# Loading w1 in two transfers and making h1 in two passes, with w2's large blocks in front of its small transfers

## The chip, the cores and the metric

The kernel runs on one core of one Trainium2 chip. The metric is device time in microseconds (us) for one execution. Before the change it is 670.66 us, the median of 3 runs (670.47 to 671.0).

## The reference: one decode step of attention and a small MLP

Four sequences (B = 4) each decode one token of width D = 640. There are two parts, each behind a layer norm and each added to its input:

```
h  = x + A(layernorm(x))        A: q = ln(x) @ wq, 32 heads of 128, softmax(q k^T / sqrt(128)) v, then @ wo
out = h + B(layernorm(h))       B: h1 = ln(h) @ w1 + b1;  act = h1 * tanh(softplus(h1));  act @ w2
```

The cached keys and values have 4096 positions for each of 32 heads and 4 sequences, in bf16: they make nearly all of the 283 MB that are read. w1 is 640 x 1728 (2160 KB), w2 is 1728 x 640. The change lies in part B alone.

## The kernel before, in words

**Attention.** The work is cut into NG = 32 groups; a group is four heads of one sequence. `load_k` and `load_v` (line 98) fetch 4 MB of keys and 4 MB of values for a group into two buffers each. For every group VectorE multiplies the keys by the query (line 348), TensorE sums the products with an identity matrix (line 355), VectorE finishes the sums (line 367), ScalarE makes the exponentials (line 398), and TensorE multiplies them by the values (line 255). Groups overlap: the values of group g - 1 are used while the keys of group g are multiplied. The last group's values come in four transfers of 1 MB (VP = 4).

All loads are issued by SyncE (SP) in program order. The schedule is written out by hand: each engine executes its instructions in the order in which the program names them.

**The loads of part B** stand behind the group loop. `w12` is one tile in the key buffer that group 30 leaves; its first columns are `w1_sb` (5 row blocks of 128 rows, side by side: `p c f`), and the rest is `w2_sb`, three large blocks of w2 (640 KB each, four rows of w2 to a partition). What is left of w2 goes to two small tiles, `w2s_sb` (128 rows, 160 KB) and `w2r_sb` (64 rows, 80 KB). SP issues w1 whole (line 476), w2s (line 477), w2r (line 478), and then the three blocks of w2 (line 480).

**The end of attention** comes next: the last exponentials, the last products with the values (lines 255 and 282), the normalisation (line 305), the last part of the product with wo (line 329), and the sum with x, `hT` (line 505). All of this holds the activations transposed, 640 features as five blocks of 128 partitions by 4 sequences.

**The MLP.** `column_means` (lines 509 and 513) gives the mean; `h2T` and `hc` are the centred activations (line 520). The product with w1 (line 534) takes h2T before it is divided by the standard deviation; that division follows later. It has FC = 14 chunks of columns: 13 of 128 and a last one, `C2`, of 64. For each chunk five matmuls (dc = 0 to 4, one for each row block of w1) sum into four columns of `h1_ps`. So the first chunk already needs all of w1. Chunks 0 to 11 read w1's columns with a stride of four elements (`f_chunk`), chunks 12 and 13 read them side by side. After chunk 4 come the two float32 matmuls of the variance (line 513); ScalarE takes its square root (line 544) and loads the table of the exponential (line 547). Then a chain without overlap runs: VectorE scales and adds b1 (lines 550, 557), ScalarE's exponential (line 565), and four VectorE instructions (lines 567 to 581) give `act_t`. The product with w2 (line 596) has 70 matmuls that sum into `y2T`: w2s first, then w2r, then the twelve chunks of the large blocks. The residual (line 604), a transposition (line 611), a copy (line 619) and the store (line 620) end the kernel.

Of the kernel before, what the change touches and what calls it, by code (L numbers as in the profile page):

```python
# [8 lines left out]
FP32 = mybir.dt.float32  # L9
BF16 = mybir.dt.bfloat16  # L10
ACT = mybir.ActivationFunctionType
# [5 lines left out]
def kernel(  # L17
# [24 lines left out]
    nc = tc.nc  # L42
# [3 lines left out]
    F = B_w1.shape[1]  # L46
    N = B * Sq
    DC = D // 128
# [19 lines left out]
    CI = 4  # L68
    CK = F // (128 * CI)
    FM = CK * CI * 128  # L70
    C2 = F // 128
    FREM = F - C2 * 128
    FC = C2 + 1

    ctx.enter_context(tc.manual_schedule())

# [49 lines left out]
    eps_t = consts.tile([128, 1], FP32)  # L126
# [9 lines left out]
    nc.gpsimd.memset(rs2[:, :, :], 0.0)  # L136
    b1T = consts.tile([128, FC], FP32)
    nc.gpsimd.memset(b1T[:, :], 0.0)
    otn = consts.tile([128, HQ, N, G], BF16)

    for q in range(G):
        nc.vector.tensor_copy(
            out=sel[:, :, q, q * PH : (q + 1) * PH],
            in_=ident[0:N, 0:N].unsqueeze(2).to_broadcast([N, N, PH]),
# [81 lines left out]
    for hq in Q_AT[-1]:  # L226
# [12 lines left out]
        out=pick[:, :],  # L239
        in_=ident_f[:, :].rearrange("p (t i) -> p i t", t=T)[:, 0 : J * G, :],  # L240
# [73 lines left out]
    def f_chunk(rows, c):  # L314

        if c < CK * CI:
            k, i = divmod(c, CI)
            block = rows[:, k * 128 * CI : (k + 1) * 128 * CI]
            return block.rearrange("p (f i) -> p i f", i=CI)[:, i, :], 128
        return rows[:, c * 128 : min(F, (c + 1) * 128)], min(F - c * 128, 128)  # L320
# [87 lines left out]
    for g in range(NG):  # L408
# [33 lines left out]
        if g in WO_AT:  # L442

            if not wo_sb:
# [3 lines left out]
                out=wo_sb[0][:, h0 : h0 + WOC, :],  # L448
                in_=A_wo.rearrange("(h p) n -> p h n", p=128)[:, h0 : h0 + WOC, :],
# [3 lines left out]
        if g == B1_AT:  # L453
            b_ps = ps.tile([128, FC], FP32, tag="small", name="b_ps")
            for c in range(FC):
                cols, fw = f_chunk(b1_row[:, :], c)
                nc.tensor.matmul(
                    b_ps[0:fw, c : c + 1],
                    lhsT=cols,
                    rhs=ident[0:1, 0:1],  # L460
                    start=True,
                    stop=True,
                )
            nc.vector.tensor_copy(out=b1T[:, 0:C2], in_=b_ps[:, 0:C2])
            nc.vector.tensor_copy(out=b1T[0:FREM, C2:FC], in_=b_ps[0:FREM, C2:FC])


    mlp = ctx.enter_context(tc.tile_pool(name="mlp", bufs=1))
    w12 = kpool.tile([128, DC * F + CK * CI * D], BF16, tag="kt", name="w12")
    w1_sb = w12[:, 0 : DC * F].rearrange("p (c f) -> p c f", c=DC)  # L470
    w2_sb = w12[:, DC * F :].rearrange("p (k i n) -> p k i n", k=CK, i=CI)
    w2s_sb = mlp.tile([128, D], BF16)
    w2r_sb = mlp.tile([FREM, D], BF16)

    w2_view = B_w2[0:FM, :].rearrange("(k p i) n -> p k i n", k=CK, i=CI)
    nc.sync.dma_start(out=w1_sb, in_=B_w1.rearrange("(c p) n -> p c n", p=128))
    nc.sync.dma_start(out=w2s_sb[:, :], in_=B_w2[FM : C2 * 128, :])
    nc.sync.dma_start(out=w2r_sb[:, :], in_=B_w2[C2 * 128 : F, :])
    for k in range(CK):
        nc.sync.dma_start(out=w2_sb[:, k], in_=w2_view[:, k])  # L480

    h1_ps = ps.tile([128, FC, N], FP32, tag="qq", name="h1_ps")
    nc.vector.memset(h1_ps[FREM:128, FC - 1, :], 0.0)

# [15 lines left out]
    dummy = consts.tile([N, 1], FP32)  # L500
# [6 lines left out]
    def column_means(src, name):  # L507
        part = mlp.tile([128, N], FP32, name=f"{name}_part")
        nc.vector.tensor_reduce(
            out=part[:, :], in_=src[:, :, :].rearrange("p c n -> p n c"), axis=AX.X, op=ALU.add  # L510
        )
        m_ps = ps.tile([128, N], FP32, tag="small", name=f"{name}_ps")
        nc.tensor.matmul(m_ps[:, :], lhsT=mean_f[:, :], rhs=part[:, :], start=True, stop=True)
        return m_ps

    m_ps = column_means(hT, "mean")
    h2T = mlp.tile([128, DC, N], BF16)
    hc = mlp.tile([128, DC, N], FP32)
    for dst in (h2T, hc):
        nc.vector.tensor_tensor(  # L520
            out=dst[:, :, :],
# [4 lines left out]
    sq = mlp.tile([128, DC, N], FP32)  # L526
# [1 line left out]


    rstd = mlp.tile([128, N], FP32)  # L530
    for c in range(FC):
        fw = f_chunk(w1_sb[:, 0, :], c)[1]
        for dc in range(DC):
            nc.tensor.matmul(  # L534
                h1_ps[0:fw, c, :],
                lhsT=f_chunk(w1_sb[:, dc, :], c)[0],
                rhs=h2T[:, dc, :],
                start=(dc == 0),
                stop=(dc == DC - 1),
            )  # L540
        if c == 4:
            v_ps = column_means(sq, "var")
            std = mlp.tile([128, N], FP32)
            nc.scalar.activation(
                out=std[:, :], in_=v_ps[:, :], func=ACT.Sqrt, bias=eps_t[:, :], scale=1.0
            )
            nc.scalar.activation(out=dummy[:, :], in_=eps_t[0:N, :], func=ACT.Exp)
            nc.vector.reciprocal(out=rstd[:, :], in_=std[:, :])
    h1n = mlp.tile([128, FC, N], FP32)
    nc.vector.tensor_tensor(  # L550
        out=h1n[:, :, :],
# [6 lines left out]
        out=h1s[:, :, :],  # L558
# [9 lines left out]
        out=tb[:, :, :],  # L568
# [8 lines left out]
        out=ta[:, :, :], in0=tb[:, :, :], scalar1=-0.5, scalar2=-1.0, op0=ALU.mult, op1=ALU.add  # L577
# [4 lines left out]
        out=act_t[:, :, :],  # L582
# [5 lines left out]
    )  # L588

    y2T = ps.tile([128, DC, N], FP32, tag="ot", name="y2T")  # L590
    w2_of = [(w2s_sb[:, :], CK * CI), (w2r_sb[:, :], C2)]
    w2_of += [(w2_sb[:, c // CI, c % CI, :], c) for c in range(CK * CI)]
    for i, (w2, c) in enumerate(w2_of):
        rows = 128 if c < C2 else FREM
        for dc in range(DC):
            nc.tensor.matmul(  # L596
                y2T[:, dc, :],
                lhsT=w2[:, dc * 128 : (dc + 1) * 128],
                rhs=act_t[0:rows, c, :],
                start=(i == 0 and dc == 0),  # L600
                stop=(i == FC - 1 and dc == DC - 1),
# [3 lines left out]
        out=oT[:, :, :].rearrange("p n c -> p c n"),  # L605
# [7 lines left out]
        lhsT=oT[:, :, :].rearrange("p n c -> p (n c)"),  # L613
        rhs=ident[:, :],
        start=True,
        stop=True,
# [35 lines left out]
```

## Time and profile before

| What | Value |
|---|---|
| median of 3 runs | 670.66 us (670.47 to 671.0) |
| time of the profiled execution | 670.71 us |
| its span, first to last instruction | 668.9 us |
| granted TensorE clock, mean | 0.838 |
| read from HBM | 283.35 MB, 424 GB/s over the span |
| busy share: TensorE, VectorE, ScalarE | 66%, 53%, 17% |

The span leaves out 1.81 us of the time of the profiled execution, which lie around the first and the last instruction. All places in time below count from the start of the span. In an instruction's row the first number is its start, the second the time that the group took, "xN" the number of instructions in it; "SPq" is SP issuing a transfer, and a row "DMA" in the chain of waits is the time from the issue of a transfer to its landing.

### The profile page before, as it was taken

How to read it: one execution, taken by the hardware profiler on the slowest of the kernel's cores; microseconds unless marked ns; L12 is line 12 of the kernel's file. 1: busy time of each engine (PE TensorE's matmuls, PEld its weight loads, DVE VectorE, ACT ScalarE, POOL GpSimd, SP SyncE). 2: the span in 40 equal slices, each digit the busy share in tenths (PEclk: the TensorE clock that was granted, in tenths of full speed). 3: DMA queues.
4: the chain of work that ended last, by engine and by line, in shares of the span. 5: the costliest groups of instructions: out<-in, count | busy, mean ns of one | idle time of the engine just before them, and what ended most of it. 6: DMA issues, size and time to landing. Idle time of an engine off the chain costs nothing.

```text
span 668.9 us, 6865 instructions
## 1 busy us (share of the span) xinstructions
PE 440.6 (66%) x2969; PEld 200.7 (30%) x2969; DVE 353.0 (53%) x306; ACT 113.8 (17%) x345; POOL 2.4 (0%) x13
## 2 busy tenths in 40 slices
PE   0588777887667475367666857757555875667775
PEld 0233333343222232133222323323222332223335
DVE  2486445556655356236654545657454566545732
ACT  0022122131111111011110111111011121111131
POOL 1000000000000000000000000000000000000000
PEclk9997889797777886797777789778788797788985
DMA  9999999999999999999999999999999999999995
GB/s 375 437 436 435 424 429 437 434 434 427 430 437 432 427 422 418 443 423 434 431 428 433 434 436 430 427 433 436 434 431 428 435 434 435 436 426 426 436 415 211
DMA packets 15478, 283.80 MB, mean 424 GB/s; under 512 B 1299, under 2 KB 5591, under 8 KB 6616
## 3 DMA queue, kind: packets, MB, share of 16 engines
q1 hardware_dynamic: 15440, 283.36, 98.8%
q8 instruction: 23, 0.38, 0.2%
q14 instruction: 7, 0.06, 0.0%
q10 hardware_dynamic: 8, 0.01, 0.0%
HBM read 283.35 MB, written 0.01 MB: 424 GB/s over the span
## 4 chain that ended last, share of the span: by engine, by line
DMA 63%; DVE 17%; PE 17%; issue 1%; SPq 0%; ACT 0%; DVEq 0%
DMA kt<-in_A_k_cache_dram 59%; DVE kt L348 15%; PE s L355 14%; DMA w<-in_B_w_dram 4%; DVE s_sb L367 2%; PE tr L380 1%; PE p_ps L255 1%; PE h_ps L534 0%; DVE mx L385 0%; PE q_ps L193 0%; PE tr L393 0%; PE y2T L596 0%; PE qb_ps L207 0%; SPq L98 0%; ACT q_all L200 0%
## 5 line engine op out<-in xcount | busy, mean ns | idle before, releaser
L355 PE MATMUL s<-kt,ident 128*128 128x512 bf16 x1024 | 296.8, 442 | 196.3 <-DVE kt L348 193.1
L348 DVE TENSOR_TENSOR kt<-kt,qbs 128x4096 bf16<-128x4096 bf16 x128 | 291.5, 2279 | 240.1 <-DMA kt<-in_A_k_cache_dram 240.1
L355 PEld LDWEIGHTS <-ident 128*128 128x128 bf16 x1024 | 110.1, 111 | 342.2 <-issue 170.6
L398 ACT ACTIVATE e<-s_sb,nbs 32x128 bf16<-32x128 f32 x128 | 74.0, 578 | 2.5
L255 PE MATMUL p_ps<-vt,e 128*16 128x512 bf16 x1016 | 64.5, 397 | 1.2 <-DMA vt<-in_A_v_cache_dram 1.2
L395 ACT COPY nbs<-tr 128x4 f32<-128x4 f32 x32 | 5.2, 162 | 331.2 <-PE tr L393 331.2
L265 ACT COPY p_sb<-p_ps 128x512 f32<-128x512 f32 x32 | 18.8, 586 | 159.7 <-PE p_ps L255 159.7
L367 DVE TENSOR_REDUCE s_sb<-s 128x64 f32<-128x512 f32 x64 | 43.5, 680 | 3.8 <-PE s L355 3.8
L271 PEld LDWEIGHTS ot<-pick,p_sb 128*128 128x128 f32 x256 | 34.3, 196 | 6.2 <-ACT p_sb L265 1.9
L255 PEld LDWEIGHTS <-e 128*16 128x16 bf16 x1016 | 23.1, 91 | 40.2 <-issue 20.0
L398 ACT ACTIVATION_READ_ACCUMULATOR e<-s_sb,nbs 32x1 f32 x128 | 32.2, 252 | 0.0
L271 PE MATMUL ot<-pick,p_sb 128*128 128x4 f32 x256 | 31.4, 246 | 0.9 <-ACT p_sb L265 0.7
L385 DVE TENSOR_REDUCE mx<-tr 1x4 f32<-1x128 f32 x32 | 8.9, 278 | 24.3 <-PE tr L380 24.3
L193 PE MATMUL q_ps<-wq_sb,xT 128*4 128x512 bf16 x40 | 11.0, 409 | 9.8 <-DMA wq_sb<-in_A_wq_dram 9.8
L380 PE MATMUL tr<-ident_f,pm 128*1 128x128 f32 x64 | 15.6, 335 | 1.2 <-DVE pm L378 1.2
L393 PEld LDWEIGHTS tr<-mx,nscale 1*128 1x128 f32 x64 | 9.4, 182 | 13.8 <-issue 12.3
L302 DVE RECIPROCAL rl<-l_ps 128x16 f32<-128x16 f32 x8 | 2.1, 258 | 21.0 <-PE l_ps L294 21.0
L207 PE MATMUL qb_ps<-q_all,sel 4*128 4x128 bf16 x128 | 9.2, 225 | 5.3 <-ACT q_all L200 5.3
L393 PE MATMUL tr<-mx,nscale 1*128 1x4 f32 x64 | 12.2, 258 | 0.4 <-DVE mx L385 0.4
L207 PEld LDWEIGHTS <-sel 4*128 4x128 bf16 x128 | 8.4, 98 | 9.1 <-issue 9.1
L200 ACT CAST q_all<-q_ps 4x512 bf16<-4x512 f32 x8 | 4.6, 575 | 35.0 <-PE q_ps L193 35.0
L380 PEld LDWEIGHTS tr<-ident_f,pm 128*1 128x1 f32 x64 | 2.8, 81 | 23.3 <-issue 23.3
(81 smaller groups left out, 69.5 us busy)
## 6 DMA issues: line engine op xcount, KB each, us to landing
kt<-in_A_k_cache_dram SPq DMA_DIRECT2D x31, 4096.0 KB, 25.2
vt<-in_A_v_cache_dram SPq DMA_DIRECT2D x31, 4096.0 KB, 32.8
wq_sb<-in_A_wq_dram SPq DMA_DIRECT2D x1, 5120.0 KB
wo_sb<-in_A_wo_dram SPq DMA_DIRECT2D x4, 1280.0 KB, 30.1
kt<-in_A_k_cache_dram SPq DMA_DIRECT2D x2, 2048.0 KB, 17.5
vt<-in_A_v_cache_dram SPq DMA_DIRECT2D x4, 1024.0 KB, 20.1
w<-in_B_w_dram SPq DMA_DIRECT2D x1, 2160.0 KB, 28.3
w<-in_B_w_dram SPq DMA_DIRECT2D x3, 640.0 KB, 16.0
```

The lines of the kernel that those rows point to most:

```text
L193: nc.tensor.matmul(q_ps[:, :], lhsT=xT[:, c, :], rhs=wq_sb[:, c, n * QC : (n + 1) * QC], start=(c == 0), stop=(c == DC - 1),)
L207: nc.tensor.matmul(qb_ps[:, b * Dh : (b + 1) * Dh], lhsT=sel[:, b, q, :], rhs=q_all[:, h * Dh : (h + 1) * Dh], start=(q == 0), stop=(q == ...
L255: nc.tensor.matmul(p_ps[c0 : c0 + J * G, :], lhsT=e2[g % NE2][:, r : r + J, :].rearrange("p j q -> p (j q)"), rhs=vts[g][:, r : r + J, :]. ...
L265: nc.scalar.copy(out=blocks[g][:, :], in_=p_ps[:, :])
L271: nc.tensor.matmul(o, lhsT=p_sb[:, j * Dh : (j + 1) * Dh], rhs=pick[:, j * G : (j + 1) * G], start=(j == 0), stop=(stop and j == J - 1),)
L348: nc.vector.tensor_tensor(out=kt[:, :, d0 : d0 + DQ], in0=kt[:, :, d0 : d0 + DQ], in1=qbs[:, hq, b, d0 : d0 + DQ].unsqueeze(1).to_broadcas ...
L355: nc.tensor.matmul(s_ps[:, :, :], lhsT=ident[:, :], rhs=kt[:, :, d : d + W], start=(d == 0), stop=(d == Dh - W),)
L367: nc.vector.tensor_reduce(out=s_sbs[g][:, part * RP : (part + 1) * RP], in_=s_of.pop((g, part))[:, :, :], axis=AX.X, op=ALU.add,)
L380: nc.tensor.matmul(tr_ps[0:1, 0:128], lhsT=pm[:, :], rhs=ident_f[:, :], start=True, stop=True)
L385: nc.vector.tensor_reduce(out=mx[:, :], in_=tr_ps[0:1, 0:128].rearrange("o (a b) -> o a b", a=G), axis=AX.X, op=ALU.max,)
L393: nc.tensor.matmul(nb_ps, lhsT=nscale[:, :], rhs=mx[:, :], start=True, stop=True)
L398: nc.scalar.activation(out=e2[g % NE2][p0:p1, :, q], in_=s_sb[p0:p1, :], func=ACT.Exp, bias=nb[p0:p1, q : q + 1], scale=SCALE, accum_out=r ...
```

## The change

w1 is loaded in two transfers, row blocks 0 to 2 (1296 KB) and 3 to 4 (864 KB). h1 is made in two passes over all chunks, the first with row blocks 0 to 2, the second with 3 and 4; both sum into the same columns of `h1_ps`, and now only the first matmul of all has the start mark and only the last has the stop mark. In each pass the chunk of 64 columns comes second, behind chunk 0. The variance stays behind chunk 4, in the first pass. SP issues the three large blocks of w2 in front of w2r and w2s, and the product with w2 takes them in that order.

```diff
+    W1_PARTS = ((0, 3), (3, DC))
...
-    nc.sync.dma_start(out=w1_sb, in_=B_w1.rearrange("(c p) n -> p c n", p=128))
-    nc.sync.dma_start(out=w2s_sb[:, :], in_=B_w2[FM : C2 * 128, :])
-    nc.sync.dma_start(out=w2r_sb[:, :], in_=B_w2[C2 * 128 : F, :])
+    w1_view = B_w1.rearrange("(c p) n -> p c n", p=128)
+    for c0, c1 in W1_PARTS:
+        nc.sync.dma_start(out=w1_sb[:, c0:c1], in_=w1_view[:, c0:c1])
     for k in range(CK):
         nc.sync.dma_start(out=w2_sb[:, k], in_=w2_view[:, k])
+
+    nc.sync.dma_start(out=w2r_sb[:, :], in_=B_w2[C2 * 128 : F, :])
+    nc.sync.dma_start(out=w2s_sb[:, :], in_=B_w2[FM : C2 * 128, :])
...
-    for c in range(FC):
-        fw = f_chunk(w1_sb[:, 0, :], c)[1]
-        for dc in range(DC):
-            nc.tensor.matmul(
-                h1_ps[0:fw, c, :],
-                lhsT=f_chunk(w1_sb[:, dc, :], c)[0],
-                rhs=h2T[:, dc, :],
-                start=(dc == 0),
-                stop=(dc == DC - 1),
-            )
-        if c == 4:
-            v_ps = column_means(sq, "var")
...
+    for c0, c1 in W1_PARTS:
+        for c in (0, C2, *range(1, C2)):
+            fw = f_chunk(w1_sb[:, 0, :], c)[1]
+            for dc in range(c0, c1):
+                nc.tensor.matmul(
+                    h1_ps[0:fw, c, :],
+                    lhsT=f_chunk(w1_sb[:, dc, :], c)[0],
+                    rhs=h2T[:, dc, :],
+                    start=(dc == 0 and c == 0),
+                    stop=(dc == DC - 1 and c == C2 - 1),
+                )
+            if c0 == 0 and c == 4:
+                v_ps = column_means(sq, "var")
...
-    w2_of = [(w2s_sb[:, :], CK * CI), (w2r_sb[:, :], C2)]
-    w2_of += [(w2_sb[:, c // CI, c % CI, :], c) for c in range(CK * CI)]
+    w2_of = [(w2_sb[:, c // CI, c % CI, :], c) for c in range(CK * CI)]
+    w2_of += [(w2r_sb[:, :], C2), (w2s_sb[:, :], CK * CI)]
```

More of the change, by code (lines that the diff above doesn't have):

```diff
@@ L530 @@
     rstd = mlp.tile([128, N], FP32)
-    for c in range(FC):
-        fw = f_chunk(w1_sb[:, 0, :], c)[1]
-        for dc in range(DC):
-            nc.tensor.matmul(
-                h1_ps[0:fw, c, :],
-                lhsT=f_chunk(w1_sb[:, dc, :], c)[0],
-                rhs=h2T[:, dc, :],
-                start=(dc == 0),
-                stop=(dc == DC - 1),
-            )
-        if c == 4:
-            v_ps = column_means(sq, "var")
[L543 to L548, printed above, removed]
+    for c0, c1 in W1_PARTS:
[11 more added lines that the diff above has]
+                v_ps = column_means(sq, "var")
+                std = mlp.tile([128, N], FP32)
+                nc.scalar.activation(
+                    out=std[:, :], in_=v_ps[:, :], func=ACT.Sqrt, bias=eps_t[:, :], scale=1.0
+                )
+                nc.scalar.activation(out=dummy[:, :], in_=eps_t[0:N, :], func=ACT.Exp)
+                nc.vector.reciprocal(out=rstd[:, :], in_=std[:, :])
     h1n = mlp.tile([128, FC, N], FP32)
```

## The prediction, made before the changed kernel was run

> **What bounds the kernel now.** I read the page first, for what fills the span.
>
> ```profile
> span 668.9 us, 6865 instructions
> DMA  9999999999999999999999999999999999999995
> HBM read 283.35 MB, written 0.01 MB: 424 GB/s over the span
> ```
>
> The DMA engines are full in every slice of the 40 but the last. The change moves no byte more or less, so nothing can be won in the first 39. Only the last 17 us are open. For these I read the chain of waits, in order of time:
>
> ```profile
> 630.11 28.26 DMA w<-in_B_w_dram
> 658.37 0.05 issue
> 658.42 0.96 PE h_ps L534 x25
> 659.38 0.43 PE var_ps L513 x2
> 659.81 1.63 PE h_ps L534 x45
> 661.44 0.02 issue
> 661.47 0.23 DVE h1n L550
> ...
> 663.26 0.23 DVE act_t L581
> 663.49 0.04 issue
> 663.53 2.20 PE y2T L596 x70
> 665.74 0.02 issue
> 665.76 0.23 DVE oT L604
> ```
>
> w1 lands at 630.11 + 28.26 = 658.37. From there to the end no transfer is waited for: 3.02 us of h1, 2.07 us of activation, 2.20 us of w2, and the store. The chain shows only what ended last. How long h1's other operand had been ready is in the timeline, together with w2's matmuls one tile at a time:
>
> ```profile
> 656.81 0.17 DVE L520 TENSOR_TENSOR h2T<-hT,mean_ps 128x20 bf16<-128x20 f32 x1 [0.68 <-PE mean_ps L513]
> 663.53 0.27 PE L596 MATMUL y2T<-act_t,w2s_sb 128*128 128x4 bf16 x5 [2.11 <-DVE act_t L581]
> 663.74 0.29 PE L596 MATMUL y2T<-act_t,w2r_sb 64*128 64x4 bf16 x5
> 663.96 1.76 PE L596 MATMUL y2T<-act_t,w 128*128 128x4 bf16 x60
> ```
>
> h2T is ready at 656.98, so TensorE waits 1.4 us for w1 alone. What SP issues, and what the transfers do at the very end (stretch, its length, busy time of PE, PEld, DVE, ACT, POOL, clock, DMA share, GB/s):
>
> ```profile
> 630.58 12.17 SPq L477 DMA_DIRECT2D w2s_sb<-in_B_w_dram  x1
> 642.80 2.12 SPq L478 DMA_DIRECT2D w2r_sb<-in_B_w_dram  x1
> 644.97 5.61 SPq L480 DMA_DIRECT2D w<-in_B_w_dram  x3
> ```
>
> ```profile
> 663.00:663.25 0.25, 0.00 (x0) 0.00 (x0) 0.23 (x1) 0.00 (x0) 0.00 (x0) 0.50 0.10 41
> 663.25:663.50 0.25, 0.00 (x0) 0.00 (x0) 0.22 (x1) 0.00 (x0) 0.00 (x0) 0.50 0.00 0
> ```
>
> SP is held for 12 us at w2s, far ahead of need. The last bytes of w2 move just before 663.25, when TensorE is about to begin with w2: behind w1, w2 is the next thing that can be late.
>
> **When the parts land.** By issue plus time to landing the last quarter of the values lands at 629.6 + 23.1 = 652.7, w1 at 658.37, w2s at 630.58 + 28.3 = 658.9, w2r at 642.80 + 16.4 = 659.2, w2's first two blocks at 645.0 + 15.7 = 660.7 and 645.9 + 16.3 = 662.2. The third's landing is not listed; one block takes 1.5 us, so it lands at about 663.7, which suits the windows. w1's 2160 KB take 5.6 us, so the last two fifths take 2.3 us, and the first part should land at 656.1. This is 0.9 us before h2T, so the first pass waits for VectorE and no longer for a transfer. The second part lands where w1 did, 658.4.
>
> **Start of h1.** A matmul follows the VectorE instruction that releases it by 0.05 us (act_t ends at 663.49, y2T begins at 663.53). So the first pass begins at 657.03 in place of 658.42: 1.39 us earlier.
>
> **The work in the two passes.** The 70 matmuls stay, and the two of the variance. In the first pass 18 matmuls, about 0.8 us with the switches below, stand before the variance, so it begins at 657.85, after its input (var_part, ready at 657.51). The first pass (42 matmuls of 0.03 us and 0.43 us for the variance, plus switches) ends at about 659.05, 0.6 us after the second part of w1 has landed: this covers the second wait. If the cover were gone, each 0.1 us of late w1 would cost 0.1 us.
>
> The order of the chunks costs something. Before, TensorE goes from 128-column weights to the 64-column chunk once, at the end, and the way back hides under the activation. Now it goes there and back in each pass, four switches in the open, three more. What one costs, w2's rows show: 60 matmuls in 1.76 us, the last taking 0.166, are 0.027 apart. Seventy at this pace would take 2.03 us; they take 2.19 (663.53 to 663.96 + 1.76), with two switches between 128 and 64 rows in them. That is 0.08 us each, and 0.24 us for three. The lower end is 0, if the weight load hides (a switch can't give time back). The upper is h1's own switch: its last 45 matmuls take 1.76 us, of which 35 strided ones (0.033 apart by the first 25 in 0.96: 1.16 us), 5 dense ones (0.13) and the last one's 0.19 us leave 0.28 for the switch and four steps of at least 0.027, so at most 0.17 us each, 0.51 for three. I take 0.08, the row that holds two whole switches.
>
> The Trainium skill, page "TensorEngine Tiling (Array Packing)", section "Tiling Modes", says that a change of the tiling mode drains TensorE, which speaks against this order of chunks. If a drain were a whole matmul of this trace (0.166 us, an estimate), three would cost 0.5 us and the gain would be 0.26 us smaller than by the row taken.
>
> **The activation** stays at 2.07 us. Its exponential needs the table that follows the variance: the variance ends at about 658.45, square root and table load (0.28 and 1.29 in the timeline) and the 0.2 us dummy end at 660.25, and the exponential is due at 660.8. So nothing comes from there.
>
> **w2.** h1 ends 1.39 - 0.24 = 1.15 us earlier, at 660.29, and y2T begins at 662.39. The queue has the same bytes and one transfer more. w2s (160 KB) lands 0.51 us after w1, w2r (80 KB) 0.3 to 0.4 after that, a 640 KB block takes 1.5: a line through these gives some 0.15 us for a transfer without bytes. In the new order the blocks land at 659.9, 661.4 and 662.9, w2r at 663.3 and w2s at 663.7 to 663.9. They are needed at 662.4, 662.9, 663.5, 664.1 and 664.3. Each is there, the third block and w2s with 0.4 to 0.6 us to spare. Moving w2s and w2r behind the blocks so costs nothing, but the cover is thin. SP issues seven transfers in place of six. The second part of w1 now stands where w2s was held for 12 us; issued at 642.8, it is still 8 us ahead of any engine's need, since the first engines run dry at 658.5 and the last at 663.2, so they reach w1's second part no earlier than 651. The last issue ended at 650.6 and may slip by 0.4 us (a w1 issue takes 0.43), with 7 us in hand. Nothing is queued behind it on SP but the store.
>
> The page "DMA: Bandwidth & Descriptors", section "Rules for kernel authors", asks for at least 1 MiB in a transfer, and the second part of w1 is under that. Its section on the anatomy of one DMA gives about 2 us of fixed time to each. If that came on top for the new transfer, w2s would land at 665.7, y2T would end at 666.1, and the kernel would be some 0.4 us slower; back-to-back transfers in this trace show 0.15.
>
> **The clock.** It is 0.50 from 650 to the end. A stretch at 0.50 with TensorE busy 2.80 of 3.41 us (343.17 to 346.58) is followed by 1.00; one with 2.19 (657.20 to 660.61) is not. Now the stretch from 657.20 would be busy for 3.1 us, so w2's matmuls may run at 1.00. Twenty such matmuls (L329) took 0.65 us at 1.00 and 0.68 at 0.50; 70 would save 0.09 us. I take it; the other end is 0, and a loss is left out, since 0.50 is the lowest clock in these rows.
>
> **Sum:** 1.39 - 0.24 + 0.09 = 1.24 us. The profiled execution took 670.71 us, 0.05 above the median; from the median it is 670.66 - 1.24 = 669.4 us.
>
> A measurement here tells 0.2%, 1.34 us, from no change. The forecast lies just inside this line, so the two outcomes are near even.
>
> **Rivals.**
>
> *The switches cost next to nothing.* h1 gains the whole 1.39 us, with the clock 1.48: 669.2 us, over the line. For it: weight loads mostly overlap matmuls. Against it: w2's two gaps. Chance 0.09.
>
> *The landing of w2s is the new bound.* If the queue's tail stretches by 1 us, y2T ends 0.35 us after w2s (five matmuls and the wait), and half of the gain is gone: 670.0 us. Against it: the same bytes. Chance 0.08.
>
> *The split does not split.* If the first pass waited for both transfers, h1 would begin at 658.42 and pay the switches: 670.9 us. Against it: w1 and w2's blocks are one tile too, and h1 began 0.05 us after w1, before any block had landed. Chance 0.05.
>
> *Slower: SP's queue.* If the wait at a full queue (12.17 us at w2s) recurs at each later transfer, w2s is issued after the engines have run dry. It decides when the last issue comes after 658.5, 8 us later than now, and costs 1 us for each further us, behind 0.4 us of cover; one more hold of 12 us gives 670.66 - 1.24 + 12 - 8 - 0.4, about 673 us. Against it: later issues took 1 to 4 us. With others that I do not see, 0.07.
>
> **How the numbers follow.** The forecast has 0.71: its gain of 1.24 us, with 0.3 us to each side for the switches (0 to 0.51), the clock (0 to 0.09) and the 0.3 us by which runs differ from their median. It lies 0.1 us inside the line, so 0.33 of this falls beyond it and 0.38 within. Faster is 0.33 + 0.09 = 0.42, within 0.2% is 0.38 + 0.08 + 0.05 = 0.51, slower 0.07. The forecast's own range is 669.0 to 669.9. The wider one, 668.9 to 670.6, takes in the cheap switches (669.2 less 0.3) and the late w2s (670.0) with more lateness than its 1 us, and leaves out the slower rival and the split that doesn't split.
>
> **What would show it.** Right: h_ps's first matmul 0.05 us after h2T, 1.4 us of wait on w gone; four gaps of 0.1 us around the 64-column chunk; h1n 1.15 us earlier; y2T's 70 matmuls without a stop; w2s's landing off the chain. Wrong: a wait for a transfer before the second pass, or inside y2T, or a first pass released by w1 and not by h2T.

## The result and the profile after

The changed kernel takes 669.6 us (median of 21 runs, 669.21 to 669.9), the kernel before 670.61 us in as many runs beside it. The ratio is 0.9985, with a 95% interval of 0.9979 to 0.9991: 1.0 us, or 0.15%, faster. The forecast was 669.4 us.

The page shows a DMA stream as full as before, over a span 1.1 us shorter. The profiled execution took 669.71 us.

```profile
span 667.8 us, 6866 instructions
DMA  9999999999999999999999999999999999999995
HBM read 283.35 MB, written 0.01 MB: 424 GB/s over the span
```

The chain of waits of the changed kernel, in order of time:

```profile
629.03 21.12 DMA vt<-in_A_v_cache_dram
...
656.75 0.18 DVE h2T L525
656.93 0.04 issue
656.98 0.97 PE h_ps L541 x18
657.94 0.43 PE var_ps L518 x2
658.37 1.91 PE h_ps L541 x52
660.31 0.23 DVE h1n L557
...
662.10 0.23 DVE act_t L588
662.33 0.04 issue
662.37 2.20 PE y2T L603 x70
664.60 0.23 DVE oT L611
```

No transfer of part B is in it any more. It now comes from the third quarter of the last values, through the end of attention, to h2T. The timeline shows what releases the first matmul of h1, and that w2's matmuls run through:

```profile
656.98 0.97 PE L541 MATMUL h_ps<-h2T,w 128*128 128x4 bf16 x18 [0.26 <-DVE h2T L525]
662.37 1.74 PE L603 MATMUL y2T<-act_t,w 128*128 128x4 bf16 x60 [2.10 <-DVE act_t L588]
664.04 0.29 PE L603 MATMUL y2T<-act_t,w2r_sb 64*128 64x4 bf16 x5
664.27 0.29 PE L603 MATMUL y2T<-act_t,w2s_sb 128*128 128x4 bf16 x5
```

SP's queue and the end of the transfers (in the windows the last two numbers are DMA share and GB/s, the third from the end is the granted clock):

```profile
629.98 3.78 SPq L480 DMA_DIRECT2D w<-in_B_w_dram  x2
633.80 13.33 SPq L482 DMA_DIRECT2D w<-in_B_w_dram  x3
647.73 1.56 SPq L484 DMA_DIRECT2D w2r_sb<-in_B_w_dram  x1
650.17 0.34 SPq L485 DMA_DIRECT2D w2s_sb<-in_B_w_dram  x1
665.49 0.32 SPq L627 DMA_DIRECT2D out_dram<-out_bf  x1
```

```profile
662.75:663.00 0.25, 0.25 (x15) 0.25 (x13) 0.00 (x0) 0.00 (x0) 0.00 (x0) 0.50 0.03 10
663.00:663.25 0.25, 0.25 (x15) 0.25 (x13) 0.00 (x0) 0.00 (x0) 0.00 (x0) 0.50 0.00 0
```

SP is held for 3.3 us at the second part of w1, which is issued by 633.8, and then for some 13 us at the blocks of w2 (8.7 us at the first); the last issue ends at 650.5 as before. w2s lands at 650.17 + 13.2 = 663.4 and is used at 664.27.

### The profile page after: what moved, and what is told of

It reads as the page before. It is cut to its first block, busy times and chain, and to the rows that moved or that the text cites. A ratio compares the mean times of both kernels' runs of the same rounds, so it can differ in the third digit from the quotient of the medians.

```text
span 667.8 us, 6866 instructions
## 1 busy us (share of the span) xinstructions
PE 443.8 (66%) x2969; PEld 201.1 (30%) x2969; DVE 353.2 (53%) x306; ACT 113.8 (17%) x345; POOL 2.4 (0%) x13
## 4 chain that ended last, share of the span: by engine, by line
DMA 62%; PE 19%; DVE 17%; issue 1%; ACT 0%; SPq 0%; DVEq 0%; ACTq 0%
DMA kt<-in_A_k_cache_dram 59%; PE s L357 15%; DVE kt L350 14%; DMA vt<-in_A_v_cache_dram 3%; DVE s_sb L369 2%; PE p_ps L257 1%; PE tr L382 1%; PE h_ps L541 0%; PE ot L273 0%; DVE mx L387 0%; PE q_ps L195 0%; PE y2T L603 0%; PE qb_ps L209 0%; PE tr L395 0%; ACT q_all L202 0%
## 5 line engine op out<-in xcount | busy, mean ns | idle before, releaser
L357 PE MATMUL s<-kt,ident 128*128 128x512 bf16 x1024 | 299.9, 446 | 192.5 <-DVE kt L350 189.3
## 6 DMA issues: line engine op xcount, KB each, us to landing
w<-in_B_w_dram SPq DMA_DIRECT2D x1, 1296.0 KB, 25.9
```

The costliest lines, as they stand in the source:

```text
L357: nc.tensor.matmul(s_ps[:, :, :], lhsT=ident[:, :], rhs=kt[:, :, d : d + W], start=(d == 0), stop=(d == Dh - W),)
```

## The experiments

Each run is compared with the kernel before on the same chip. Two theories stood against each other. "Overlap" says that the gain is h1's earlier start less the switches of the weights' shape. "Tail" says that w2's landings set the end, so that w2's order wins the time.

**The split without w2's new order.** In the changed kernel, both the transfers and the matmuls of w2 go back.

```diff
+    nc.sync.dma_start(out=w2s_sb[:, :], in_=B_w2[FM : C2 * 128, :])
+    nc.sync.dma_start(out=w2r_sb[:, :], in_=B_w2[C2 * 128 : F, :])
     for k in range(CK):
         nc.sync.dma_start(out=w2_sb[:, k], in_=w2_view[:, k])
-    nc.sync.dma_start(out=w2r_sb[:, :], in_=B_w2[C2 * 128 : F, :])
-    nc.sync.dma_start(out=w2s_sb[:, :], in_=B_w2[FM : C2 * 128, :])
...
-    w2_of = [(w2_sb[:, c // CI, c % CI, :], c) for c in range(CK * CI)]
-    w2_of += [(w2r_sb[:, :], C2), (w2s_sb[:, :], CK * CI)]
+    w2_of = [(w2s_sb[:, :], CK * CI), (w2r_sb[:, :], C2)]
+    w2_of += [(w2_sb[:, c // CI, c % CI, :], c) for c in range(CK * CI)]
```

> The changed kernel with w2's transfers and matmuls back in their old order (w2s, w2r, then the three blocks). Theory 'overlap': the gain is h1's earlier start less three switches of the weights' shape, and w2's order plays no part, since in the changed kernel the last transfer lands at 663.39 and is wanted at 664.27. So 669.6 us as with the whole change, a ratio of about 0.9985 to the kernel before, y2T's 70 matmuls in 2.2 us without a stop; the third block, wanted at about 664.0, lands at about 663.4. Rival 'tail': w2's landings set the end once h1 is earlier, and the new order wins the time. Then y2T waits inside for a block, and the time is 670.0 to 670.6 us.

Measured: 669.7 us, ratio 0.9985 [0.9976, 0.9993], the same as the whole change. Its chain has y2T in one piece, 2.22 us in place of 2.20:

```profile
662.38 2.22 PE y2T L602 x70
```

So the gain is there without w2's new order, and "tail" is refuted for this kernel.

**w2's new order without the split.** The same edit the other way round, in the kernel before.

> The kernel before with w2's new order alone: w1 whole, one pass. Overlap: 670.6 us, ratio 1.000, within 0.05%; h1 still waits for w1 until about 658.4. Tail: some 0.3 to 0.6 us faster, since the large blocks land earlier.

Measured: 670.3 us beside 670.7, ratio 0.9994 [0.9985, 1.0003]. The median is 0.4 us lower, which the interval does not settle; "overlap" had expected 0.05% at most. The trace shows where such a gain would come from, and it is not where "tail" looked. The chain of this run:

```profile
630.03 27.93 DMA w<-in_B_w_dram
658.00 0.97 PE h_ps L535 x25
```

w1 itself lands at 657.96, not at 658.37. I formed a third theory, "neighbours": what follows w1 in the queue sets how fast w1's last part moves. The windows of 1 us, the kernel before first, then this run:

```profile
656.00:657.00 1.00, 0.59 (x2) 0.50 (x2) 0.32 (x3) 0.00 (x0) 0.00 (x0) 0.50 1.08 392
657.00:658.00 1.00, 0.00 (x0) 0.00 (x0) 0.43 (x3) 0.00 (x0) 0.00 (x0) 0.50 1.02 388
```

```profile
656.00:657.00 1.00, 0.59 (x2) 0.50 (x2) 0.32 (x3) 0.00 (x0) 0.00 (x0) 0.50 1.02 420
657.00:658.00 1.00, 0.00 (x1) 0.01 (x1) 0.44 (x3) 0.00 (x0) 0.00 (x0) 0.50 1.03 424
```

The DMA engines are about as busy in both, and move 8% more with the large blocks behind w1 than with the small transfers, whose rows are 1280 B.

**The new issue order alone, matmuls in the old order,** to test that. In the kernel before only the lines of w2's transfers are reordered.

> The kernel before with w2's transfers issued in the new order, and its matmuls left in the old one (w2s and w2r first). The new order of both without the split measured 670.3 us, 0.3 to 0.4 us under the kernel before, against the expectation of none: in its profile w1 landed at 657.95 in place of 658.37. Theory 'neighbours': the rows of 1280 B of w2s and w2r, moved beside the last of w1, cost bandwidth (in 656 to 658 us 377 to 392 GB/s with the old order, 412 to 424 with the new one), so w1 lands 0.3 to 0.4 us earlier wherever large blocks follow it: 670.3 us, w1 at 658.0. Rival 'matmul order': the gain comes from the product with w2, or is scatter: 670.6 us, w1 at 658.3.

Measured: 670.52 us, ratio 0.9999 [0.999, 1.0008]. The time fits the rival, but the chain shows a wait of its own that hides w1's earlier landing:

```profile
649.47 13.80 DMA w2s_sb<-in_B_w_dram
663.32 2.22 PE y2T L597 x70
```

w1 landed early here too (h1's first matmul is at 657.98), as "neighbours" says. But w2's product still asks first for w2s, which now is the last to land, and it waited until 663.32 although act_t was ready at 663.05. My expectation had overlooked this wait. It takes back 0.27 us; the 0.21 us by which y2T still begins ahead of the kernel before (663.53) do not show in the medians, 670.52 beside 670.56. So w1's earlier landing is seen in both runs that reorder the transfers of a whole w1, and in this one most of it is lost because the matmuls do not follow the transfers' order. Whether the order is worth 0.4 us by the clock on the wall stays unsettled by its interval. In the changed kernel the old order gave the same time (669.7 and 669.6 us), since h1 no longer waits for w1.

**w1 in one transfer, two passes.**

```diff
-    for c0, c1 in W1_PARTS:
-        nc.sync.dma_start(out=w1_sb[:, c0:c1], in_=w1_view[:, c0:c1])
+    nc.sync.dma_start(out=w1_sb, in_=w1_view)
```

> The changed kernel with w1 in one transfer: two passes stay, w2's new order stays. Overlap: h1 starts with w1's landing as before and pays the three extra switches: 0.25 to 0.3 us slower than before, about 670.9 us, ratio 1.0004; h1 takes 3.3 us from its first matmul to its end in place of 3.0. Rival 'passes': a second pass over the same columns of the accumulator costs something of its own, then clearly over 0.3 us slower; if the passes are free, 670.6 us.

Measured: 670.62 us, ratio 1.0 [0.9991, 1.0009]. The timeline:

```profile
651.66 1.05 PE L273 MATMUL ot<-pick,p_sb 128*128 128x4 f32 x8 [0.74 <-ACT p_sb L267]
655.77 0.17 DVE L524 TENSOR_TENSOR h2T<-hT,mean_ps 128x20 bf16<-128x20 f32 x1 [0.68 <-PE mean_ps L517]
658.07 1.00 PE L540 MATMUL h_ps<-h2T,w 128*128 128x4 bf16 x18 [2.34 <-DMA w<-in_B_w_dram]
659.36 2.03 PE L540 MATMUL h_ps<-h2T,w 128*128 128x4 bf16 x52
```

h1 takes 3.32 us (658.07 to 661.39) in place of 3.02, as expected. The time missed the expected 670.9 us: w1 landed at 658.02 here, 0.35 us ahead of the kernel before, as "neighbours" says, and this nearly cancels the 0.3 us. A price of the second pass itself, beyond the switches, shows neither in the time nor in h1's row. Without the split there is no gain.

**w1 in two transfers, one pass.**

```diff
-    nc.sync.dma_start(out=w1_sb, in_=B_w1.rearrange("(c p) n -> p c n", p=128))
+    w1_view = B_w1.rearrange("(c p) n -> p c n", p=128)
+    for c0, c1 in ((0, 3), (3, DC)):
+        nc.sync.dma_start(out=w1_sb[:, c0:c1], in_=w1_view[:, c0:c1])
```

> The kernel before with w1 in two transfers and nothing else: h1 in one pass, w2's old order. This is the price of one more transfer in the queue. Overlap: 670.6 to 670.75 us, ratio 1.000 to 1.0002, the second part landing at about 658.4. By the 2 us of fixed time for each transfer that the Trainium skill's page 'DMA: Bandwidth & Descriptors' (Anatomy of one DMA) states, it would be an estimated 672.6 us if the queue ran empty in between.

Measured: 670.46 us, ratio 0.9999 [0.999, 1.0007]; the second part landed at 631.42 + 26.73 = 658.15. One more transfer in a full queue has no price that can be measured here: the interval, 0.1% to each side or some 0.6 us, rules out 2 us and cannot tell 0.15 us from nothing. One pass gains nothing from the split, since chunk 0 needs the last row block.

**The 64-column chunk once.** In the changed kernel it leaves both passes, and all its five matmuls stand at the end.

```diff
-        for c in (0, C2, *range(1, C2)):
+        for c in range(C2 if c0 == 0 else FC):
...
-            for dc in range(c0, c1):
+            for dc in range(c0 if c < C2 else 0, c1):
...
-                    start=(dc == 0 and c == 0),
-                    stop=(dc == DC - 1 and c == C2 - 1),
+                    start=(dc == 0 and c in (0, C2)),
+                    stop=(dc == DC - 1 and c >= C2 - 1),
```

> The changed kernel with the 64-column chunk out of both passes: all its five matmuls stand at the end of the second pass, as before the change. One switch of the weights' shape in the open in place of four, the same 70 matmuls. Overlap with switches at 0.08 us each: 0.25 us faster than the whole change, 669.35 us, a ratio of about 0.9981; h1 takes 3.0 us. If switches cost nothing: 669.6 us, and the 0.28 us that h1 grew by have another cause, the passes themselves.

Measured: 669.44 us, ratio 0.9984 [0.9975, 0.9993]: 0.16 us under the changed kernel's median. This lies between the two expectations, 669.35 and 669.6, and does not decide between them; h1's own time does. The chain is from an execution of 670.47 us, in which the clock fell early (last section):

```profile
652.98 1.87 PE ot L273 x8
657.75 0.19 DVE h2T L525
657.98 0.63 PE h_ps L541 x15
658.61 0.55 PE var_ps L518 x2
659.16 1.97 PE h_ps L541 x55
661.15 0.23 DVE h1n L557
```

h1 takes 3.15 us (657.98 to 661.13) in place of 3.30. The variance holds the chain for 0.55 us in place of 0.43: it now stands behind 15 matmuls and waits 0.12 us for its input. Without this wait h1 would take 3.03 us, and before the change it took 3.02; so the three switches cost the 0.28 us. The single matmuls of the changed kernel's timeline say the same: on the way to the 64-column chunk two starts lie 0.10 us apart (657.04 and 657.14), on the way back 0.13 (657.26 and 657.39), in the second pass again 0.10 and 0.13 (659.03 to 659.13, 659.21 to 659.34), against 0.03 between matmuls of 128 columns. So going there adds 0.07 us, coming back 0.10.

**One switch in each product.** On top of that, w2r goes to the end of w2's transfers and matmuls, so that no weights of 128 rows follow it.

> As the run with the 64-column chunk once, and w2r (64 rows) moved to the very end, behind w2s, in SP's queue and among w2's matmuls, so that w2's product too has one switch in place of two. Overlap: another 0.08 us, 669.27 us, ratio 0.998; y2T takes 2.1 us in place of 2.2. Tail: no gain, since the last transfer then stops y2T; y2T begins at about 662.1 and wants w2r at about 664.0, and it lands at about 663.4.

Measured: 669.27 us, ratio 0.9979 [0.997, 0.9988]. In its profile h2T was ready at 656.04, 0.9 us earlier than in the changed kernel, and two waits came up that the changed kernel does not have:

```profile
658.19 1.35 PE L541 MATMUL h_ps<-h2T,w 128*128 128x4 bf16 x31 [0.15 <-DMA w<-in_B_w_dram]
663.13 0.70 PE L603 MATMUL y2T<-act_t,w 128*128 128x4 bf16 x20 [0.28 <-DMA w<-in_B_w_dram]
```

The second pass waits for w1's second part, and y2T for w2's third block, so the 2.1 us expected for y2T did not come in this profile. Here "tail" holds: once the end of attention is 0.9 us faster, w2's landing is the bound.

**The variance behind chunk 6** in place of chunk 4, on top of the last run.

> As the run with one switch each, but with the variance behind chunk 6 in place of chunk 4. With the 64-column chunk out of the first pass only 15 matmuls stand ahead of the variance, and in that run's trace the gap between the 15th matmul and the variance's end is 0.59 us in place of 0.46: TensorE waits 0.13 us for the variance's input. Overlap: that wait goes, 669.27 - 0.13 = 669.15 us. Tail: w2's third block already stopped y2T in the run with one switch each (0.44 us in its middle, in a profile whose clock fell late), so nothing is won where the clock falls late; then 669.2 to 669.3 us.

Measured: 669.21 us, ratio 0.998 [0.9971, 0.9988]. This is within 0.1 us of both expectations, 669.15 and 669.2 to 669.3, and does not decide between them. The chain:

```profile
656.99 0.82 PE h_ps L541 x21
657.81 0.43 PE var_ps L518 x2
658.25 1.76 PE h_ps L541 x49
660.03 0.23 DVE h1n L557
...
662.10 2.11 PE y2T L603 x70
```

h1 takes 3.02 us (656.99 to 660.01), the 0.12 us of wait are gone, and y2T takes 2.11 us with its one switch in place of two.

**Fillers that stream many columns.** The changed kernel has twelve matmuls of 512 columns added in TensorE's gaps; the trace shows nine of them.

```diff
+    fill_ps = ps.tile([128, RP, W], FP32, tag="s", bufs=2, name="fill_ps")
+
+    def fill(n):
+        for _ in range(n):
+            nc.tensor.matmul(
+                fill_ps[:, :, :],
+                lhsT=ident[:, :],
+                rhs=qbs[:, 0, :, :].rearrange("p b d -> p (b d)"),
+                start=True,
+                stop=True,
+            )
...
```

> The changed kernel with twelve matmuls of 512 columns put into TensorE's idle gaps of the last 18 us (3 ahead of the last quarters of the values, 1 ahead of the add of the blocks, 1 ahead of the last part of the product with wo, 2 and 1 around the mean, 4 ahead of w2); their sums go to an accumulator that nobody reads. They test what raises the granted clock. In the changed kernel a stretch filled to 91% with matmuls of 4 columns (651.91 to 655.33) was not followed by 1.00. Theory 'columns': streamed columns raise it, busy time doesn't. Then it is 1.00 from about 652 on; the eight float32 matmuls of the blocks' add take 0.95 us in place of 1.87, mean and variance about half, and the end comes 0.5 to 1.2 us earlier (w2s lands at 663.4 and limits it), 668.5 to 669.1 us. Rival 'phase': the stretches' phase decides, and fillers only delay: the clock stays at 0.50, each filler takes 0.43 us, and the kernel is 0 to 1.5 us slower than the whole change.

Measured: 669.54 us, ratio 0.9993 [0.9983, 1.0003], inconclusive as a time: six of eleven executions took 668.98 to 669.54 us and five 671.05 to 672.0. Neither theory expected two groups, and only two of the six reach the 669.1 us of "columns". The profile is of one of the six, and y2T waits 0.44 us in it for w2's third block. The clock's changes lie 3.41 us apart in this profile, at 649.02, 652.43 and 655.84, and so the windows have this length; the changed kernel first, then this run:

```profile
648.50:651.91 3.41, 1.50 (x16) 0.12 (x8) 0.00 (x0) 0.58 (x1) 0.00 (x0) 0.50 1.01 418
651.91:655.33 3.42, 3.10 (x54) 3.04 (x55) 0.17 (x1) 1.49 (x3) 0.00 (x0) 0.50 1.02 411
655.33:658.74 3.41, 2.66 (x50) 2.48 (x47) 1.02 (x7) 0.31 (x2) 0.00 (x0) 0.50 1.00 411
```

```profile
649.02:652.43 3.41, 2.88 (x16) 0.70 (x13) 0.00 (x0) 0.77 (x2) 0.00 (x0) 0.50 1.01 415
652.43:655.84 3.41, 3.10 (x65) 2.57 (x66) 0.54 (x3) 1.30 (x2) 0.00 (x0) 1.00 1.03 418
655.84:659.25 3.41, 3.41 (x69) 3.12 (x68) 0.81 (x5) 1.53 (x2) 0.00 (x0) 0.50 0.95 387
```

In the changed kernel 3.10 us of busy TensorE, nearly all matmuls of 4 columns, are not followed by 1.00. In this run 2.88 us with fillers are. That fits "columns", in one profile. The run with the 64-column chunk once has a harder case (windows of 3 us):

```profile
645.00:648.00 3.00, 2.86 (x24) 1.28 (x16) 0.26 (x1) 2.25 (x7) 0.00 (x0) 0.50 1.02 430
648.00:651.00 3.00, 3.00 (x24) 2.02 (x27) 0.00 (x0) 0.00 (x0) 0.00 (x0) 0.50 1.00 416
```

TensorE was busy for 5.86 of these 6 us, about 3.5 us of them with matmuls of 512 columns, and the clock stayed at 0.50 all the same. So busy time alone doesn't raise the clock; how many columns are needed in a stretch, and what its phase does, these runs leave open.

What the five longer executions do was not profiled. The recorded clock, a mean over the whole span, is 0.828 to 0.836 in them and 0.835 to 0.843 in the six, which leans to a clock that stayed low. But the kernel before varies as much without two groups of times, so this is not shown.

**Fillers on top of the run with one switch each.**

> The fillers on top of the run with one switch each. Columns: as the fillers alone and up to 0.3 us less, unless the last transfer limits both; then the two agree and y2T waits inside. Phase: 0 to 1.5 us slower than the run with one switch each.

Measured: 668.99 us, ratio 0.9983 [0.9974, 0.9992]; eight of eleven executions took 668.78 to 669.2 us, three 670.75 to 671.05. The eight fit "columns", the three do not. It has the lowest median of all runs, but not the steadiest time. Of the versions without fillers, the ones at 669.21 and 669.27 us are the best. All three lie under the changed kernel's 669.6, and their intervals against the kernel before overlap with its interval.

## Why the prediction was right, point by point

- **What bounds the end.** The step "the first pass waits for VectorE and no longer for a transfer" holds: h1's first matmul is released by h2T, 0.05 us after it. The first part of w1 landed at 630.0 + 25.9 = 655.9, against 656.1.
- **Start of h1.** Predicted 1.39 us earlier, measured 658.42 - 656.98 = 1.44; h2T's own place is 0.06 us earlier in this profile.
- **Switches.** Predicted 0.24 us (0 to 0.51), measured 3.30 - 3.02 = 0.28. That the chunk's order is the cause, and not the second pass, is shown by the runs that keep both passes and put the chunk at the end: h1 takes 3.02 us with the variance behind chunk 6, and 3.03 without its wait with the variance behind chunk 4. The rule of the Trainium skill that a change of tiling mode drains TensorE ("TensorEngine Tiling (Array Packing)", "Tiling Modes") points at such a cost. Whether TensorE drains here no run shows; the measured 0.07 and 0.10 us are less than the whole matmul taken there as an estimate (0.166).
- **The cover of the second wait** held: the second part landed at 630.5 + 27.4 = 657.9, the first pass ended at about 659.
- **The transfer more.** Taken at 0.15 us, measured at nothing that can be told from zero. The fixed 2 us of the page "DMA: Bandwidth & Descriptors" (its anatomy of one DMA) are given there for transfers that GpSimd issues; these are SP's, in a full queue, and the run with two transfers and one pass, 670.46 us, rules out 2 us for them. SP's hold did not stand at w1's second part, as predicted, but mostly at w2's first block; nothing waited for it.
- **w2.** The three blocks were predicted for 659.9, 661.4 and 662.9, and the first and the third landed at 633.8 + 25.7 = 659.5 and 645.3 + 17.6 = 662.9. No wait arose.
- **The clock: this term failed.** The step "the stretch from 657.20 would be busy for 3.1 us, so w2's matmuls may run at 1.00" gave 0.09 us; measured nothing, the clock stays at 0.50. It counted busy time without asking what fills it. The windows above show a stretch of 3.10 busy us of small matmuls that lifts nothing. In the row that I had read the rule from, seven matmuls of 512 columns filled 2.80 us. It also took the stretches to begin where they did in the profile before (where the clock fell at 650.4, a little behind the 650 of the prediction). In the profile after the clock fell at 648.50, and steps of 3.41 us from there cut h1's work at 658.74, into 1.76 and 1.54 us; the stretch of 3.1 us did not arise.
- **The sum.** 1.44 - 0.28 + 0 = 1.16 us, and the store is issued 1.16 us earlier (665.49 in place of 666.65). Of these the profiled executions keep 1.00 (669.71 in place of 670.71); the other 0.16 us are lost behind the store and around the span, and are of the size by which executions differ. The median gained 1.01. Without the clock the prediction's sum was 1.15; that it was met so closely is partly luck, as the start was 0.05 us better and the switches 0.04 us worse. The prediction called the two sides of its line at 1.34 us near even, so that the gain stayed under the line says little; the rows say more.

The rival of free switches fell with h1's time in the chunk's runs, the late w2s, the unsplit split and the held queue with the profile after. All four pieces of the change are now placed: two transfers and two passes give the gain together and nothing apart, the chunk's order takes 0.28 us back, and w2's order is not needed here.

## What to carry to other kernels

Where an engine waits for a large load whose first part would do, split load and work together, and read the gain from the gap between the other operand and the landing, less what the second pass adds in switches. Put matmuls of another weight shape at one end of a sequence, where the way back hides under the next wait. After each such gain look for the next landing in line: here 0.9 us more would already have made w2 the bound.

## What the runs showed that I had not expected

**The phase of the clock moves the end of attention.** h2T is ready at 655.94 in one profile, at 656.92 in the changed kernel's and at 657.92 in another, with the values landing alike. For the first two the rows of the eight float32 matmuls that add up the last blocks (line 273) tell most of it: they take 1.05 us where the clock is still at 1.00 at 651.7, and 1.87 us at 0.50. In the third the clock fell to 0.50 at 644.7 already, in the changed kernel at 648.5. There these eight take 1.87 us too, but they begin at 652.98 in place of 651.97, since the products with the values ahead of them ended later. The kernel before does not feel this, since it waits for w1 in any case: in the run with one transfer h2T came at 655.94, and h1 began at 658.07. The changed kernel, which waits for h2T, would: in the run with the 64-column chunk once the profiled execution has h2T 1.0 us late and took 670.47 us, 1.03 over its median. None of the 21 executions of the changed kernel itself was as late (669.21 to 669.9).

**Small transfers behind a load slow its last part.** With w2s and w2r behind w1, the DMA engines moved 392 and 388 GB/s in the two microseconds from 656, with the large blocks there 420 and 424, at the same busy share; a whole w1 landed 0.35 to 0.45 us later with the small transfers behind it. Two more profiles with the small transfers next (the old order of w2 in the changed kernel, two transfers with one pass) show 370 to 382 GB/s there. With w1 split the landing moves less: 658.15 and 658.3 in these two, 657.9 in the changed kernel. Whether the short rows or the number of transfers cost it was not tried.
